# Soft-MoE attention kernel: batch-end rows stored by one transfer of 128 rows, two and a half early half-groups, last weight slab in row pieces of 4, 2, 1, 1

## Chip, cores, metric

One core of a Trainium2 chip. The metric is the device time of one execution in microseconds (us). Before the change: 181.42 us, median of 3 runs (181.19 to 181.47).

## The reference, cut to what matters

```python
attn_out = attention(q, k, v)                       # 8 batches, 8 heads, 576 tokens, 64 per head
x = attn_out.transpose(0, 2, 1, 3).reshape(4608, 512)
logits = x @ phi                                    # 32 slots: 8 experts of 4
slot_input = softmax(logits, over tokens).T @ x     # needs all tokens
for e in range(8):                                  # two matrices of 512 x 1024 for each expert
    slot_out[e] = relu(slot_input[e] @ w1[e]) @ w2[e]
return softmax(logits, over slots) @ slot_out       # 4608 x 512 float32, 9.4 MB
```

The output, 9.44 MB, can only be computed when the last expert's `w2` has arrived. So the kernel ends with a long stretch of stores: after about 150 us.

## The kernel before

Words used below: PE is the matmul engine (PEld its weight loads); DVE, ACT and POOL are the vector, scalar and GpSimd engines; SP issues the stores. SBUF is the on-chip memory of 128 partitions that the stores read, HBM the memory that they write. "DMA engines" are the 16 engines that move the data of all transfers.

The kernel computes attention batch by batch while a queue of transfers brings q, k, v and then the weights (cast to bf16 on the way). The last expert weights come as column slabs (`s` = 0 or 1: columns 0 to 255, 256 to 511), so that the left half of the output can start before the right half's weights are there:

```python
for s in range(2):
    wq += [w2_slab(6, s), w2_slab(7, s, 0, 4), w2_slab(7, s, 4, 2),
           w2_slab(7, s, 6, 2)]        # expert 7 in row pieces of 4, 2, 2
...
for x in (1, 2):                       # left, right columns
    l2((6,), x, ...)                   # matmuls with w2 of expert 6
    for y, cs in enumerate((range(4), range(4, 6), range(6, 8))):
        l2((7,), x, 256 * x - 256, 256, cs, [b_w2h[y][x - 1]])
    op(DVE, ... tensor_tensor(o_so ..., AluOp.add) ...)        # "the add" below, line 881
```

The output is then made in tiles of 128 tokens: one matmul, one eviction (ACT or DVE, in turn, copies the result to a float32 staging area in SBUF), and stores from there. Each batch has 576 = 512 + 64 tokens. A *group* G of 0 to 7 is the first 512 tokens of a batch: partition p holds tokens 4p to 4p + 3, so one row in memory is 4 x 2 KB = 8 KB, and the group is one 1 MB transfer of 128 rows. The eight *batch ends* of 64 tokens are gathered as a ninth group, 16 partitions for each batch, and stored by eight transfers:

```python
def tok(G, j):                                        # the columns (tokens) of tile j of group G
    return (a(o_et + 576 * G + j, [[4, 128]]) if G < 8 else a(o_tail + j, [[4, 128]]))

NA = 2                                                # groups 0, 1: stored by column halves
def store(G, c0, cw, prio, j0=0, n=4):
    for p0 in [0] if G < 8 else range(0, 128, 16):
        pn = 128 if G < 8 else 16
        dst = out[576 * G:576 * G + 512] if G < 8 else out[36 * p0 + 512:36 * p0 + 576]
        ...                                           # SP issues the transfer
```

Groups 0 and 1 are stored early: their left halves (four transfers of 256 KB, two tiles each, 1 KB rows) while the right slab of `w2` is still loading, their right halves after it. Then come group 2 (two transfers of 512 KB, 4 KB rows), groups 3 to 7 (1 MB each, 8 KB rows), and last the eight batch-end stores of 128 KB.

The softmax here doesn't subtract the row's maximum and nothing guards it: scores larger than these inputs give would overflow.

## Time and profile before

| | before |
|---|---|
| time, median | 181.42 us |
| span of the profiled run | 179.8 us |
| last weights landed | 152.3 us |
| add of the right half starts | 153.29 us |
| evictions done | 165.1 us |
| 8 KB packets, first start to last end | 161.24 to 178.97 us |

From the profile page of the kernel before: the span in 40 equal slices of 4.5 us. The first line is the busy share of the 16 DMA engines in tenths, the second what they moved.

```profile
DMA  5999999999999999999999999999999999799995
GB/s 184 233 210 211 214 209 213 215 208 213 213 210 215 212 209 210 215 211 208 215 211 211 215 210 214 214 214 211 215 211 213 197 196 235 243 401 408 425 346 162
```

The DMA engines are busy in nearly all slices. About 210 GB/s in the first 31 slices counts bf16 as written; the inputs that are read are float32, so twice as many bytes (the page: 30.41 MB in the load queue, 61.93 MB read from HBM). The stores then run at 400 to 425, and the last two slices fall to 346 and 162: the end of the stream is slow.

The windows view of the kernel before, for stretches of the store phase. The columns after the window are its length, then busy time and instructions of each engine, the clock granted to PE, the busy share of the DMA engines, and GB/s.

```profile
core 0: us, PE busy (x) PEld busy (x) DVE busy (x) ACT busy (x) POOL busy (x), PEclk, DMA share, GB/s
150.00:153.50 3.50, 3.25 (x18) 1.64 (x16) 1.10 (x4) 0.67 (x2) 0.00 (x0) 0.54 1.12 284
153.50:155.50 2.00, 1.73 (x12) 1.37 (x13) 1.49 (x5) 1.39 (x4) 0.00 (x0) 1.00 0.39 138
155.50:160.50 5.00, 4.84 (x18) 1.43 (x16) 5.00 (x9) 5.00 (x10) 0.00 (x0) 1.00 1.01 360
160.50:165.50 5.00, 2.29 (x8) 0.55 (x7) 4.60 (x7) 3.27 (x6) 0.00 (x0) 1.00 1.03 422
165.50:173.50 8.00, 0.00 (x0) 0.00 (x0) 0.00 (x0) 0.00 (x0) 0.00 (x0) 0.58 1.01 420
173.50:179.00 5.50, 0.00 (x0) 0.00 (x0) 0.00 (x0) 0.00 (x0) 0.00 (x0) 0.50 0.87 204
```

Read the last column. From 153.5 to 155.5 us the rate is 138: the early stores run out before the right half's stores can start. From 160.5 to 173.5 it is 420: rows of 8 KB. From 173.5 to 179 it is 204, and no compute engine has anything to do. These are the eight batch-end stores.

The transfers that write the output, from the DMA view: number, size, and median time from issue to landing.

```profile
out_dram<-ar SPq DMA_DIRECT2D x5, 1024.0 KB, 8.1
...
out_dram<-ar SPq DMA_DIRECT2D x8, 256.0 KB, 3.4
...
out_dram<-ar SPq DMA_DIRECT2D x2, 512.0 KB, 4.0
out_dram<-ar SPq DMA_DIRECT2D x8, 128.0 KB, 8.9
```

The timeline of the kernel before around the right half's add (start, length, engine, line, operation; in brackets the idle time before it and what ended it):

```profile
152.64 0.13 PEld L857 LDWEIGHTS ps<-ar 128*32 128x32 bf16 x2 [0.34 <-DMA ar<-in_moe_w_dram]
153.29 0.43 DVE L881 TENSOR_TENSOR ar<-ps,ar 64x256 bf16<-64x256 f32 x1 [2.40 <-PE ps L857]
...
153.77 9.16 PE L901 MATMUL ps<-ar 128*128 128x256 bf16 x36 [0.52 <-DVE ar L881]
```

Two matmuls (152.64) still had to run after the last weights, then the add (L881), then the output tiles (L901).

A word on packets. The trace records each packet of a transfer with its start, its time and its size; a store with 8 KB rows has one packet of 8,192 B for each row. Sorted by start, the 768 such packets fall into six blocks of 128, one for each megabyte. (The records do not name the engine that moved a packet, and the blocks are cut by count, so their borders blur where engines are apart.) In this kernel a block that runs smoothly has a mean packet of 314 to 319 ns: 128 packets on 16 engines, 8 for each on average, 2.5 us.

### The profile page before, as it was taken

How to read it: one execution, taken by the hardware profiler on the slowest of the kernel's cores; microseconds unless marked ns; L12 is line 12 of the kernel's file. 1: busy time of each engine (PE TensorE's matmuls, PEld its weight loads, DVE VectorE, ACT ScalarE, POOL GpSimd, SP SyncE). 2: the span in 40 equal slices, each digit the busy share in tenths (PEclk: the TensorE clock that was granted, in tenths of full speed). 3: DMA queues.
4: the chain of work that ended last, by engine and by line, in shares of the span. 5: the costliest groups of instructions: out<-in, count | busy, mean ns of one | idle time of the engine just before them, and what ended most of it. 6: DMA issues, size and time to landing. Idle time of an engine off the chain costs nothing.

```text
span 179.8 us, 4781 instructions
## 1 busy us (share of the span) xinstructions
PE 125.4 (70%) x2092; PEld 84.5 (47%) x2092; DVE 116.9 (65%) x219; ACT 104.9 (58%) x164; POOL 50.9 (28%) x101
## 2 busy tenths in 40 slices
PE   0008877987989899899789889885775469892000
PEld 0005645764767667666567667674431125420000
DVE  6898789779798798898699699291200104797000
ACT  2406598796798788787688788945020103794000
POOL 7559742242334134133930000951000000000000
PEclk9999999999999999999999999999999975999555
DMA  5999999999999999999999999999999999799995
GB/s 184 233 210 211 214 209 213 215 208 213 213 210 215 212 209 210 215 211 208 215 211 211 215 210 214 214 214 211 215 211 213 197 196 235 243 401 408 425 346 162
DMA packets 18900, 41.26 MB, mean 230 GB/s; under 512 B 1984, under 2 KB 8128, under 8 KB 17984
## 3 DMA queue, kind: packets, MB, share of 16 engines
q0 software_dynamic: 15024, 30.41, 89.6%
q1 hardware_dynamic: 3856, 10.55, 16.5%
q8 instruction: 16, 0.26, 0.5%
q14 instruction: 4, 0.03, 0.0%
HBM read 61.93 MB, written 9.44 MB: 397 GB/s over the span
## 4 chain that ended last, share of the span: by engine, by line
DMA 59%; DVE 20%; PE 6%; ACT 3%; issue 2%; POOL 2%; DVEq 0%
DMA ar<-in_k_dram 41%; DMA ar<-in_moe_w_dram 18%; DVE ar L488 6%; DVE ar L913 6%; DVE ar L614 2%; PE ps L857 2%; DVE ar L445 2%; PE ps L901 1%; POOL ar L371 1%; ACT ar L548 1%; DVE ar L450 1%; PE ps L509 1%; ACT ar L576 1%; ACT ar L670 1%; POOL ar L364 1%
## 5 line engine op out<-in xcount | busy, mean ns | idle before, releaser
L488 DVE STREAM_TRANSPOSE ar<-ar 128x576 uint32<-128x576 uint32 x40 | 48.5, 1239 | 7.7 <-DMA ar<-in_k_dram 7.7
L548 ACT ACTIVATE ar<-ps 128x1152 bf16<-128x1152 f32 (+1 forms) x32 | 38.0, 1186 | 20.6 <-PE ps L533 11.4
L509 PE MATMUL ps<-ar 128*128 128x320 bf16 (+1 forms) x128 | 22.7, 301 | 15.6 <-DVE ar L488 13.1
L614 DVE TENSOR_TENSOR ar<-ps,fs 96x768 bf16<-96x768 f32 (+1 forms) x32 | 26.3, 823 | 1.3
L576 ACT ACTIVATE ar<-ps 128x768 bf16<-128x768 bf16 x32 | 24.8, 810 | 2.2 <-PE ps L570 2.1
L509 PEld LDWEIGHTS ps<-ar 128*128 128x128 bf16 x128 | 10.5, 99 | 20.2 <-POOL ar L418 13.1
L570 PE MATMUL ps<-ar 128*128 128x128 bf16 x192 | 15.9, 229 | 3.8 <-DVE ar L614 3.4
L603 PE MATMUL ps<-ar 128*128 128x65 bf16 x320 | 14.7, 193 | 3.3 <-ACT ar L548 3.2
L910 ACT ACTIVATE ar<-ps,fs 128x512 f32<-128x512 f32 (+1 forms) x22 | 11.4, 656 | 8.7 <-PE ps L901 8.7
L857 PE MATMUL ps<-ar 128*32 128x512 bf16 (+1 forms) x80 | 11.7, 374 | 6.0 <-DMA ar<-in_moe_w_dram 5.4
L335 POOL DMA_DIRECT2D ar<-in_k_dram x16 | 8.9, 555 | 24.8 <-DVE ar L488 15.6
L570 PEld LDWEIGHTS ps<-ar 128*128 128x128 bf16 x192 | 12.4, 118 | 5.7 <-DVE ar L614 4.0
L603 PEld LDWEIGHTS ps<-ar 128*128 128x128 bf16 x320 | 12.0, 97 | 6.0 <-ACT ar L548 3.7
L913 DVE TENSOR_SCALAR ar<-ps,fs 128x512 f32<-128x512 f32 (+1 forms) x22 | 12.6, 649 | 1.3 <-PE ps L901 1.3
L364 POOL DMA_DIRECT2D ar<-in_moe_w_dram x12 | 6.4, 580 | 20.8 <-DVE ar L488 20.8
L335 POOL DMA_DIRECT2D ar<-in_q_dram x16 | 8.8, 547 | 10.5 <-DVE fs L610 5.0
L901 PE MATMUL ps<-ar 128*128 128x512 bf16 (+1 forms) x44 | 10.7, 372 | 1.4 <-DVE ar L881 1.1
L610 DVE RECIPROCAL fs<-ps 96x12 f32<-96x12 f32 (+1 forms) x32 | 6.2, 195 | 7.9 <-PE ps L603 7.6
L670 ACT ACTIVATE ar<-ps 128x576 bf16<-128x576 bf16 x16 | 9.6, 652 | 3.1 <-PE ps L654 3.1
L335 POOL DMA_DIRECT2D ar<-in_v_dram x16 | 8.8, 549 | 8.8 <-DVE fs L610 5.5
L857 PEld LDWEIGHTS ps<-ar 128*32 128x32 bf16 x80 | 5.0, 104 | 12.3 <-DMA ar<-in_moe_w_dram 8.8
L693 PE MATMUL ps<-ar 128*128 128x288 bf16 x64 | 9.2, 287 | 1.2 <-ACT ar L677 1.2
(75 smaller groups left out, 186.7 us busy)
## 6 DMA issues: line engine op xcount, KB each, us to landing
ar<-in_moe_w_dram POOLq DMA_DIRECT2D x29, 512.0 KB, 27.5
out_dram<-ar SPq DMA_DIRECT2D x5, 1024.0 KB, 8.1
ar<-in_k_dram POOLq DMA_DIRECT2D x16, 288.0 KB, 23.4
ar<-in_q_dram POOLq DMA_DIRECT2D x16, 288.0 KB, 23.5
ar<-in_v_dram POOLq DMA_DIRECT2D x16, 288.0 KB, 23.6
out_dram<-ar SPq DMA_DIRECT2D x8, 256.0 KB, 3.4
ar<-in_moe_w_dram SPq DMA_DIRECT2D x1, 1024.0 KB, 5.0
out_dram<-ar SPq DMA_DIRECT2D x2, 512.0 KB, 4.0
```

The source lines that it names most:

```text
L335: return pool.dma_start(a(o_stg + (s * 3 + j) * 1152, [[1, 1152]]), src[b, 4 * dl:4 * dl + 4].rearrange("h (p t) d -> (h p) (t d)", p=32))
L488: return dve.transpose(au(o_dst, [[1, 18], [18, 32]]), au(src, [[32, 18], [1, 32]]))
L509: pe.matmul(pf(h, 0, [[1, W]]), a(o_id, [[1, 128]]), a(msk, [[1, W]]), start=True, stop=False)
L548: eo = op(ACT, lambda P=P, W=W: act.activation(a(P, [[W, 4], [1, W]]), AP(ps, 0, [[4096, 128], [512, 4], [1, W]]), ACTF.Exp, scale=SCALE), ...
L570: last = pe.transpose(pb(bank.idx, bb * 256 + par * 32, [[64, 4], [1, 32]]), src, a(o_id, [[1, 128]]))
L576: op(ACT, lambda t=t, bank=bank: act.activation(a(o_vb[vs] + 3 * t * VBK, [[66, 12], [2, 32], [1, 2]]), pb(bank.idx, 0, [[64, 12], [1, 32] ...
L603: last = pe.matmul(pf(bank.idx + x, 65 * t, [[1, 65]]), w, a(VB + t * VBK + 66 * h, [[1, 65]]), start=True, stop=True)
L614: op(DVE, lambda hp=hp, bank=bank: dve.tensor_tensor(a(ox + 128 * hp, [[64, 2], [256, NT], [1, 64]], 0, rows), pf(bank.idx, 0, [[512, 2], ...
L857: last = pe.matmul(pf(sobank[x].idx, 0, [[1, n]], 32 * j, 32), a(o_htz + 1024 * g + 128 * c + 32 * j, [[1, 32]]), a(w2off(e) + DM * c + co ...
L901: op(PE, lambda: pe.matmul(pf(bank.idx, 0, [[1, cw]]), tok(G, j), a(o_so + c0, [[1, cw]]), start=True, stop=True), pet(1, cw), prio, reads ...
L910: op(ACT, lambda: act.activation(dst, src(), ACTF.Copy, scale=sca), actt(cw, .1), prio + .1, reads=[bank, b_rinv], writes=wr, name=f"OE{G} ...
L913: op(DVE, lambda: dve.tensor_scalar(dst, src(), sca, None, op0=AluOp.mult), dvet(cw, True) + .08, prio + .1, reads=[bank, b_rinv], writes= ...
```

## The change

The intent: the last stretch is taken to be slow because it consists of eight small transfers, so store all batch ends by one transfer of 128 rows of 8 KB, in the middle of the stream. Fill the hole at 154 us with a fifth early half-store ("two and a half groups by halves"). Let fewer matmuls wait for the last weights (row pieces of 4, 2, 1, 1). The diff, cut to its core:

```diff
-               w2_slab(7, s, 6, 2)]
+               w2_slab(7, s, 6, 1), w2_slab(7, s, 7, 1)]
...                                                  # POOL gathers the batch ends: partition p = 8 i + b
-        a(o_tail, [[64, 8], [1, 64]]), a(o_et + 512, [[576, 8], [1, 64]])), .8, T1 + 4, reads=[b_et],
+        a(o_tail, [[4, 8], [32, 16], [1, 4]]), a(o_et + 512, [[576, 8], [4, 16], [1, 4]])), .8, T1 + 4, reads=[b_et],
...
-        for y, cs in enumerate((range(4), range(4, 6), range(6, 8))):
+        for y, cs in enumerate((range(4), range(4, 6), range(6, 7), range(7, 8))):
...
-    NA = 2
+    NA = 2.5
...
-        for p0 in [0] if G < 8 else range(0, 128, 16):
-            pn = 128 if G < 8 else 16
-            dst = out[576 * G:576 * G + 512] if G < 8 else out[36 * p0 + 512:36 * p0 + 576]
...
+        if G < 8:
+            dst = out[576 * G:576 * G + 512, c0:c0 + cw].rearrange("(p j) f -> p j f", j=4)[:, j0:j0 + n, :]
+            src = af(ostg(G) + 2 * (512 * j0 + c0), [[512, n], [1, cw]])
+        else:
+            dst = out.rearrange("(b r) f -> b r f", b=8)[:, 512:576, :].rearrange("b (i j) f -> i b (j f)", j=4)
+            src = af(ostg(G), [[1, 2048]])
...                                                  # order: group 2, the batch ends, groups 3 to 7
+    for G, x in [(2, 2)] + [(G, x) for G in (8, 3, 4, 5, 6, 7) for x in (0, 2)]:
```

Partition 8i + b now holds tokens 4i to 4i + 3 of the end of batch b. In the destination, i (16 values, 8 KB apart) is the outer dimension and b (8 values, 1.18 MB apart) the inner one, because b and i cannot be one dimension of 128 with one step.

More of the change, by code (lines that the diff above doesn't have):

```diff
@@ L309, in bass_dilated_sliding_attn__then__soft_moe_slots_kernel @@
     b_w5h = [Buf(f"w5h{x}") for x in range(2)]
-    b_w2h = [[Buf(f"w2h{x}{s}") for s in range(2)] for x in range(3)]
+    b_w2h = [[Buf(f"w2h{x}{s}") for s in range(2)] for x in range(4)]
     b_htz, b_tail, b_so = Buf("htz"), Buf("tail"), [Buf("soA"), Buf("soB")]
@@ L373, in fn @@
                 moe_w2[e].rearrange("(p c) f -> p c f", c=8)[:, c0:c0 + n, 256 * s:256 * s + 256])
-        return (fn, n << 17, f"w2s_{e}{s}{c0}", [b_w2[e][s] if n == 8 else b_w2h[(0, 4, 6).index(c0)][s]])
+        return (fn, n << 17, f"w2s_{e}{s}{c0}", [b_w2[e][s] if n == 8 else b_w2h[(0, 4, 6, 7).index(c0)][s]])
     for e in range(8):
@@ L919, in store @@
               if c0 < 256 * (s + 1) and c0 + cw > 256 * s]
-        for p0 in [0] if G < 8 else range(0, 128, 16):
-            pn = 128 if G < 8 else 16
-            dst = out[576 * G:576 * G + 512] if G < 8 else out[36 * p0 + 512:36 * p0 + 576]
-            dst = dst[:, c0:c0 + cw].rearrange("(p j) f -> p j f", j=4)
-            store_ops.append(op(SP, lambda p0=p0, pn=pn, dst=dst: spq.dma_start(
-                dst[:, j0:j0 + n, :],
-                af(ostg(G) + 2 * (512 * j0 + c0), [[512, n], [1, cw]], p0, pn)), .1, prio, kind="dma",
-                nbytes=pn * n * cw * 4, rate=347e3 if cw < 512 else 420e3,
-                sem=sem(f"s_o{G}{c0}{j0}{p0}"), reads=rd, name=f"ST{G}{c0}{j0}{p0}"))
+        if G < 8:
[4 more added lines that the diff above has]
+            src = af(ostg(G), [[1, 2048]])
+        store_ops.append(op(SP, lambda: spq.dma_start(dst, src), .1, prio, kind="dma",
+                            nbytes=128 * n * cw * 4, rate=347e3 if cw < 512 else 420e3,
+                            sem=sem(f"s_o{G}{c0}{j0}"), reads=rd, name=f"ST{G}{c0}{j0}"))
     T2 = T1 + 40
@@ L939, in bass_dilated_sliding_attn__then__soft_moe_slots_kernel @@
         store(G, 256, 256, T2 + 10 + G + .25 * x + .2, x, 2)
-    for n in range(int(2 * NA), 18):
-        G, x = n // 2, n % 2 * 2
+    for G, x in [(2, 2)] + [(G, x) for G in (8, 3, 4, 5, 6, 7) for x in (0, 2)]:
+        at = G if G < 8 else 2.6
         for j in (x, x + 1):
-            out_tile(G, j, 0, 512, T2 + 10 + G + .25 * x)
-        if G == NA:
-            store(G, 0, 512, T2 + 10 + G + .25 * x + .2, x, 2)
+            out_tile(G, j, 0, 512, T2 + 10 + at + .1 * x)
+        if G < NA:
+            store(G, 0, 512, T2 + 10 + at + .1 * x + .1, x, 2)
         elif x:
-            store(G, 0, 512, T2 + 10 + G + .5)
+            store(G, 0, 512, T2 + 10 + at + .3)
     order = sc.run([4, 5, 6, 7], [0, 1, 2, 3], last_ex[0])
```

## The prediction

> **What bounds the kernel now.** The DMA engines: 90% busy or more in nearly all of the page's slices, and 59% of the chain of waits that ended last. They load until 152.3 us; from then on only stores are left. Store rates, by stretches of the trace:
> - first column-half stores (four of 256 KB): issued by 151.6, flowing until 155.0, below full rate from 153.5; around 155.0 to 155.5 nothing moves, because the second half's matmuls wait for the last w2 piece (152.6) and its add (153.29);
> - 1 KB rows (second halves) 348 GB/s, 4 KB rows (group 2) about 400, 8 KB rows (1 MB stores) 420, steady to 173.5;
> - then the eight batch-end stores of 128 KB[...]: 1.05 MB from 173.8 to 178.9 (208 GB/s), though six were issued by 172.2. At 420 GB/s these bytes take 2.5 us. Last landing 179.3, span 179.8.
>
> Compute ends at 165.1.
>
> **What the change does.**
> 1. One 1 MB transfer replaces the eight; its destination is 16 x 8 rows of 8 KB. [...] It moves to just after group 2, so the kernel ends with a plain 1 MB store. Worth 5.05 - 2.5 = 2.5 us, all on the path.
> 2. A fifth 256 KB store before the last w2 piece. It fills the hole of 153.5 to 155.5, where about 0.48 MB of capacity is unused. It is 0.75 us of DMA work at 348 GB/s; in return half of group 2's 512 KB store goes at 348 instead of 400 (+0.1 us). Net 0.5 to 0.8 us. It costs two matmuls (0.23 us each) before the L2 of the second half, where PE idled 0.34 us.
> 3. Row pieces 4, 2, 1, 1: one matmul, not two (0.62 us), after the last landing, 0.1 to 0.3 us off each add; this pays for point 2's delay. Two more POOL issues at 113 to 119 us, behind 30 us of queued transfers: free.
> 4. Strided batch-end copy on POOL (0.60 us now, perhaps 1): PE waits longer at 125 us, but its next weights land near 140. Free.
>
> **Sum.** Second-half stores flow from about 155.4 us; 1.31 MB at 348, 0.52 at 400, 6.29 at 420 GB/s are 20.1 us, so the last data go at 175.6 and the span ends near 176.5. Gain 3.2 us: 181.42 becomes about **178.2 us**, range 177.4 to 179.2 (8 in 10). Chances: faster by over 2% 0.30, within 2% 0.69, slower 0.01.
>
> **What would show it right or wrong.** Right: store rate near 420 GB/s until the last us; the merged store moving in about 2.5 us around 161 to 163; the rate no longer zero near 155; last add at about 153.2; compute done at about 165.
>
> **What would make it wrong.** The 128 KB stores may be slow not from their number but from where they write (128 KB in one stretch at a time); then the merged store would be slow too: 180.7. The fifth store could slow the last weight pieces and delay the add. The hole could close only on some engines, as others work until 155.0: then point 2 gives 0.3. If the second add comes earlier than I think, or the stream ends with less skew, 177.4.

The 3.2 us are 2.5 us of point 1, worked out from the rates of the trace, and about 0.7 us of point 2 (point 3 was to pay for its delay), and the sum came to 178.2 us. The recorded expectations below have cuts of the same kind.

## The result

| | before | changed |
|---|---|---|
| time, median of 6 runs each | 181.37 us | 180.80 us (180.65 to 181.03) |
| ratio of the changed to before | | 0.9972 (0.9959 to 0.9985) |
| span of the profiled run | 179.8 us | 179.0 us |
| add of the right half starts | 153.29 us | 152.95 us |
| first 8 KB packet starts | 161.24 us | 160.45 us |
| last 8 KB packet ends | 178.97 us | 178.22 us |
| between these two | 17.73 us | 17.77 us |

A ratio here and below is fast runs of one kernel over fast runs of the other in the same rounds, so it is not quite the ratio of the medians that are quoted. Executions over 1.5% slower than the fastest of the same kernel are left out of the means. The bracket is a 95% interval.

The kernel is 0.3% faster, not 1.8%. The last row of the table already says where the gain is missing: the six megabytes in 8 KB rows, which contain the batch ends in both kernels, take 17.7 us in both.

The slices of the changed kernel:

```profile
DMA  6999999999999999999999999999999999899996
GB/s 185 234 213 210 217 207 215 211 211 210 218 207 213 215 209 210 215 210 210 215 208 212 213 211 217 211 215 210 219 209 217 196 195 230 304 356 264 421 419 260
```

The end is somewhat better, but there is a new low of 264 GB/s in the fourth slice from the end. The windows view of the changed kernel, same columns and windows as before:

```profile
core 0: us, PE busy (x) PEld busy (x) DVE busy (x) ACT busy (x) POOL busy (x), PEclk, DMA share, GB/s
150.00:153.50 3.50, 2.62 (x17) 1.33 (x18) 0.94 (x3) 0.28 (x1) 0.00 (x0) 1.00 1.18 307
153.50:155.50 2.00, 1.82 (x13) 1.43 (x14) 1.61 (x5) 1.72 (x5) 0.00 (x0) 1.00 0.67 234
155.50:160.50 5.00, 4.86 (x19) 1.34 (x17) 5.00 (x10) 5.00 (x10) 0.00 (x0) 1.00 1.07 367
160.50:165.50 5.00, 1.73 (x6) 0.41 (x5) 4.00 (x7) 2.72 (x5) 0.00 (x0) 1.00 0.99 262
165.50:173.50 8.00, 0.00 (x0) 0.00 (x0) 0.00 (x0) 0.00 (x0) 0.00 (x0) 0.54 1.01 423
173.50:179.00 5.50, 0.00 (x0) 0.00 (x0) 0.00 (x0) 0.00 (x0) 0.00 (x0) 0.50 0.68 286
```

The hole (153.5 to 155.5) went from 138 to 234 GB/s, as intended. But from 160.5 to 165.5 the rate is 262 where it was 422, with the DMA engines busy all the time (0.99). That is the merged store. And the last window is not a full 420 up to a sharp end: worked out from the packet records, the rate was 425 until 176.5 us and then declined over 1.7 us. The DMA view of the changed kernel has six stores of 1 MB now, with 11.0 us from issue to landing where five had 8.1:

```profile
out_dram<-ar SPq DMA_DIRECT2D x6, 1024.0 KB, 11.0
...
out_dram<-ar SPq DMA_DIRECT2D x10, 256.0 KB, 3.8
...
out_dram<-ar SPq DMA_DIRECT2D x1, 512.0 KB, 4.0
```

The timeline of the changed kernel around the add:

```profile
151.20 1.71 PE L857 MATMUL ps<-ar 128*32 128x256 bf16 x8 [0.18 <-DMA ar<-in_moe_w_dram]
...
152.63 0.09 PEld L857 LDWEIGHTS ps<-ar 128*32 128x32 bf16 x1 [0.31 <-DMA ar<-in_moe_w_dram]
152.95 0.43 DVE L881 TENSOR_TENSOR ar<-ps,ar 64x256 bf16<-64x256 f32 x1 [2.44 <-PE ps L857]
...
153.44 1.29 PE L901 MATMUL ps<-ar 128*128 128x256 bf16 x10 [0.52 <-DVE ar L881]
...
154.92 7.41 PE L901 MATMUL ps<-ar 128*128 128x512 bf16 x25 [0.18 <-DVE ar L913]
```

The new piece of one row works: one matmul runs behind the last weights instead of two, and in this pair of profiles the add comes 0.34 us earlier, and the first tiles with it. But most of the 0.34 us is not the piece. The profile of the kernel before happened to have a granted PE clock of 0.54 from 150 to 153.5 us, the changed one 1.00 (windows above). merge_only, a run described below, keeps the two matmuls and had a clock of 1.00:

```profile
152.63 0.39 PE L857 MATMUL ps<-ar 128*32 128x256 bf16 x2 [0.29 <-DMA ar<-in_moe_w_dram]
153.06 0.43 DVE L881 TENSOR_TENSOR ar<-ps,ar 64x256 bf16<-64x256 f32 x1 [2.70 <-PE ps L857]
```

From the first of these matmuls to the add it took 0.43 us there, 0.65 in the kernel before and 0.32 in the changed one. So at the same clock the finer piece is worth 0.11 us, and the other 0.22 us belong to the clock of one profile. Evictions end 0.6 us earlier (164.5 instead of 165.1). What is left is to explain the slow merged store. Its packets (from the packet records, sorted by start, rows of 16; ns):

```
160.45  573 795 611 319 454 709 619 400 612 309 614 309 496 309 606 309
160.91  309 472 572 642 646 595 604 360 346 380 631 596 629 596 636 629
161.44  629 629 629 598 629 594 600 645 647 605 596 631 598 635 646 648
162.08  867 888 871 818 879 878 904 687 738 741 672 671 558 529 539 559
162.94  309 309 382 309 309 309 518 309 309 542 309 406 501 424 309 508
163.25  309 309 309 309 309 372 312 622 312 309 633 309 645 602 309 309
```

309 ns is the undisturbed packet, and 629 is about twice that. After a mixed start more than two rows of 16 are near 629: this looks like engines that move in step, 16 at a time, each at half its speed (inferred). A row of up to 904 ns follows, and then the pattern breaks up.

### The profile page after: what moved, and what is told of

It is laid out like the page before. It is cut to its first block, busy times and chain, and to the rows that moved or that the text cites. A ratio compares the mean times of both kernels' runs of the same rounds, so it can differ in the third digit from the quotient of the medians.

```text
span 179.0 us, 4780 instructions
## 1 busy us (share of the span) xinstructions
PE 127.9 (71%) x2093; PEld 87.5 (49%) x2094; DVE 118.0 (66%) x220; ACT 104.7 (58%) x165; POOL 51.7 (29%) x103
## 4 chain that ended last, share of the span: by engine, by line
DMA 32%; PE 23%; DVE 23%; ACT 6%; POOL 4%; issue 2%; DVEq 0%
DMA ar<-in_moe_w_dram 18%; DMA ar<-in_k_dram 15%; PE ps L509 7%; DVE ar L488 6%; DVE ar L913 6%; ACT ar L548 4%; POOL ar L371 4%; PE ps L603 3%; DVE ar L614 3%; PE ps L570 3%; PE ps L516 2%; PE ps L526 2%; PE ps L693 2%; DVE ar L494 2%; DVE ar L445 2%
## 5 line engine op out<-in xcount | busy, mean ns | idle before, releaser
L509 PE MATMUL ps<-ar 128*128 128x320 bf16 (+1 forms) x128 | 23.9, 313 | 15.4 <-DVE ar L488 13.1
L509 PEld LDWEIGHTS ps<-ar 128*128 128x128 bf16 x128 | 10.9, 102 | 20.1 <-POOL ar L418 13.1
L603 PE MATMUL ps<-ar 128*128 128x65 bf16 x320 | 15.7, 200 | 3.4 <-ACT ar L548 3.1
L603 PEld LDWEIGHTS ps<-ar 128*128 128x128 bf16 x320 | 12.9, 101 | 6.3 <-ACT ar L548 3.8
L570 PEld LDWEIGHTS ps<-ar 128*128 128x128 bf16 x192 | 12.8, 120 | 3.6 <-DVE ar L614 2.4
L857 PE MATMUL ps<-ar 128*32 128x512 bf16 (+1 forms) x80 | 10.5, 338 | 5.0 <-DMA ar<-in_moe_w_dram 3.5
L901 PE MATMUL ps<-ar 128*128 128x512 bf16 (+1 forms) x45 | 9.8, 339 | 1.5 <-DVE ar L881 1.0
```

Source lines behind the costliest of these rows:

```text
L509: pe.matmul(pf(h, 0, [[1, W]]), a(o_id, [[1, 128]]), a(msk, [[1, W]]), start=True, stop=False)
L570: last = pe.transpose(pb(bank.idx, bb * 256 + par * 32, [[64, 4], [1, 32]]), src, a(o_id, [[1, 128]]))
L603: last = pe.matmul(pf(bank.idx + x, 65 * t, [[1, 65]]), w, a(VB + t * VBK + 66 * h, [[1, 65]]), start=True, stop=True)
L857: last = pe.matmul(pf(sobank[x].idx, 0, [[1, n]], 32 * j, 32), a(o_htz + 1024 * g + 128 * c + 32 * j, [[1, 32]]), a(w2off(e) + DM * c + co ...
```

## Theories

These are conjectures; the runs below test them.

- **P, partitions.** How long a packet takes depends on which partitions are read at the same time: in some combinations the engines hold each other up. Which combinations was a guess, as no record names the engine of a packet. The measured packets would fit: plain stores have means of 314 to 319 ns; the merged store has rows of 16 near 629 ns, about 2 x 309, as if two engines took turns; the eight stores of before, which read 16 neighbours each, have 33 of their 128 packets over 900 ns, up to 1,466, as if up to four did. That the 16 x 8 form reads partitions 8 apart at the same time is part of the guess. Engines that get out of step would hold each other up less.
- **H, memory addresses.** The rows written together lie within one stretch of 128 KB (8 KB apart), or the next rows after them are 1.18 MB further on.
- **F, form.** The three-dimensional destination is itself slow.
- **N, number.** Before, eight small transfers were slow because each costs something; the merge removed that, and something else took its place.

## The experiments

Each run was timed beside fresh runs of the kernel before on the same chip (medians 181.36 to 181.55 us); runs of different rounds are best compared by their ratios to it.

### undo_merge: the change without the merged store

```diff
-    one 16 x 8 store after group 2, strided gather
+    the eight 16-row stores and the gather of before, last
```

> The fifth store and the finer weight pieces alone, with the eight batch-end stores of before, last. The trace after shows the last add 0.34 us earlier and the dip near 155 us filled, so these two parts alone should give 0.5 to 0.9 us: 180.5 to 180.9. If the merge itself gained nothing, this run is as fast as the changed kernel (180.8); if the merge gained the 0.5 us that its stretch of 4.6 us instead of 5.05 us suggests, this run is at 181.2; if the merge lost time through the uneven end that it leaves, this run is faster, 180.3.

180.95 us, ratio 0.9973 (0.9959 to 0.9987). The time is just above the expected 180.5 to 180.9. Without the merge the change is as good as with it (0.9972). The two small parts carry what was gained.

### merge_only: the merged store alone, in the kernel before

> The kernel before with only the merged batch-end store right after group 2. By the prediction alone it would be 2.5 us faster, 178.9. [...]three steps of 16 packets near 629 ns, then a mixed fourth, a stretch of 4.6 us, and an end that is uneven by 0.7 us; time 181.0 to 181.5, no different from before within 0.2%.

The second forecast is that of theory P; it carries over the packets of the changed kernel.

181.46 us, ratio 0.9994 (0.9982 to 1.0007). The merge by itself is worth nothing that can be told from noise. The blocks of 16 packets near 629 ns are there; the 8 KB packets take 17.80 us from first to last.

### fifth_only and pieces_only

```diff
-    NA = 2            # fifth_only: the kernel before, this and the condition of group 2's store
+    NA = 2.5
```

```diff
-               w2_slab(7, s, 6, 2)]      # pieces_only: the kernel before, with this and its matmuls
+               w2_slab(7, s, 6, 1), w2_slab(7, s, 7, 1)]
```

> The kernel before with only the fifth early store of 256 KB. If the hole near 155 us is what these two small parts gain from, 0.3 to 0.7 us: 180.7 to 181.1. If the gain of the run without the merge (0.47 us) came from the finer weight pieces, this run is within 0.15 us of before.

180.92 us, ratio 0.9968 (0.9955 to 0.9981).

> The kernel before with only the row pieces 4, 2, 1, 1. The add of the second half comes 0.2 to 0.3 us earlier, but the DMA engines that still work on the early stores until 155.0 do not finish sooner: 0 to 0.3 us, 181.1 to 181.4.

181.34 us, ratio 0.9993 (0.9979 to 1.0008). The fifth store alone gives all of the gain; the finer pieces bring the add a little earlier but do not clearly change the time. Both runs are inside their expected ranges.

### wide_16x8: six stores in the 16 x 8 form, rows 72 KB apart

The last six groups are all stored in the form of the merged store. In the destination the outer dimension steps by 72 KB instead of 8 KB, the inner one still by 1.18 MB. The rest of the kernel is that of pitch36 (below), so the two differ only in the form of these six stores.

```diff
+    if G > 2:
+        dst = out.rearrange("(b i g j) f -> g i b (j f)", b=8, i=16, g=9)[G]
+        src = af(ostg(G), [[1, 2048]])
```

> A wrong (permuted) result on purpose: the last six groups are all stored in the 16 x 8 form[...]. P and F: each of the six takes about 4.6 us instead of 2.5, so about 10 us slower than the changed kernel, near 191. H by closeness[...]: all fast, about 178. H by jumps of 1.18 MB: slow like P.

181.20 us, ratio 0.9990 (0.9972 to 1.0008). All four guesses missed. Against pitch36, 178.31 us, the form costs 2.9 us. (The rows of the output are so alike that the permutation is an error of 1.2%, worked out from the reference's output.) The windows of this run:

```profile
core 0: us, PE busy (x) PEld busy (x) DVE busy (x) ACT busy (x) POOL busy (x), PEclk, DMA share, GB/s
...
160.50:165.50 5.00, 1.91 (x6) 0.54 (x5) 4.08 (x7) 2.80 (x5) 0.00 (x0) 1.00 0.98 261
165.50:173.50 8.00, 0.00 (x0) 0.00 (x0) 0.00 (x0) 0.00 (x0) 0.00 (x0) 0.52 1.02 403
```

The first of the six stores is as slow as in the changed kernel (mean packet 528 ns against 518, the same steps of 16 near 629), though its rows are 72 KB apart and not 8: closeness in memory is not the cause. The second has 356 ns, the other four 316 to 322, though they have the same form and the same jumps of 1.18 MB: neither the form nor the jumps are slow in themselves. So the slowness seems to belong to engines that move in step, and to end when they have fallen out of step (inferred from the packet times, as the records do not name the engines; no run shows the drift itself). My expectation for P had left out that the slowness ends by itself after the first store or two. The end seems to pay instead: the last store took 3.7 us from first start to last end, although its mean packet was 316 ns, so some engines seem to finish late.

### merged_112: same memory rows, other partitions

Seven batch ends on 112 partitions (p = 7i + b, so one step of i is 7 partitions instead of 8), the eighth as one store of partitions 112 to 127.

```diff
-    a(o_tail, [[4, 8], [32, 16], [1, 4]])            # p = 8 i + b
+    a(o_tail, [[4, 7], [28, 16], [1, 4]])            # p = 7 i + b, b < 7
+    a(o_tail + 448, [[1, 64]])                       # p = 112 + i, b = 7
```

> Same form and same HBM rows, other SBUF partitions: seven batch ends from 112 partitions[...], and the eighth as 16 rows. Theory P [...]the 7-part transfer moves in about 2.5 us with most packets near 310 ns instead of 500 to 650, the 16-row one stays slow; the time is 0.7 to 1.2 us below the changed kernel, 179.6 to 180.1. Theory F (the 16 x n form) and theory H (HBM rows close together or 1.18 MB apart): packets stay at 500 to 650 ns, time stays 180.8 or a little worse.

180.42 us, ratio 0.9949 (0.9937 to 0.9962), 0.4 us better than the changed kernel's 180.8, less than P's 0.7 to 1.2. The packets show where. The first 96 packets have a mean of 398 ns instead of 529, and 13 of them instead of 53 are over 550 ns. The 16-row store behind it reads 16 neighbours, and eight packets there took 1,173 to 2,060 ns, which probably cost part of the gain (the longest are well over 4 x 309 ns; this stays open). Same memory rows and same kind of form, other partitions, other speed: that is for P, against H and F. Why steps of 7 are better than steps of 8 is not shown.

### halves_64: half of the partitions at a time

All-plain stores (the kernel of pitch36, below), but the last six groups are stored as two two-dimensional transfers of 64 partitions each, first the six of partitions 0 to 63, then the six of 64 to 127. Each memory row is the same.

```diff
+    part(0, 64, ...)                                 # now
+    late.append(lambda: part(64, 64, ...))           # after all groups' first parts
```

> The pitch-36 kernel (178.3 us), but the last six groups are each stored as two plain two-dimensional transfers of 64 partitions, all six of partitions 0 to 63 first, then all six of 64 to 127; same HBM rows of 8 KB, same sizes in all. Theory P: [...]packets near 620 ns, 6.3 MB at about 212 GB/s, 29.7 us instead of 14.8: about 193 us. Theories of form or of HBM addresses: packets stay near 310 to 320 ns, about 178.5.

193.02 us (one run, state unknown; the effect is 14.7 us). P had said about 193, the other theories 178.5, which is also near what pitch36 took (178.31). P's figure is an estimate, two packet times of 309 ns for every packet; why half of the partitions should double it was a guess, not shown before this run. The windows:

```profile
core 0: us, PE busy (x) PEld busy (x) DVE busy (x) ACT busy (x) POOL busy (x), PEclk, DMA share, GB/s
...
160.50:165.50 5.00, 1.90 (x6) 0.54 (x5) 4.07 (x7) 2.78 (x5) 0.00 (x0) 0.83 1.01 220
165.50:173.50 8.00, 0.00 (x0) 0.00 (x0) 0.00 (x0) 0.00 (x0) 0.00 (x0) 0.50 1.00 209
173.50:179.00 5.50, 0.00 (x0) 0.00 (x0) 0.00 (x0) 0.00 (x0) 0.00 (x0) 0.50 0.99 226
```

The engines are always busy, at half the rate: 6.29 MB from 160.5 to 190.4 us is 210 GB/s, and the means of the six blocks are 555 to 632 ns. There is no 16 x 8 form here, and no recovery like that of wide_16x8: the blocks stay slow. Nor is it the size of 512 KB: the two 512 KB stores of the kernel before, over 128 partitions, ran at about 400 GB/s (399 from 159 to 161 us).

### small_step8: the eight stores of before, with partitions 8 apart

The run without the merge, except that each 128 KB store reads partitions b, b + 8, ... b + 120 instead of 16 neighbours.

```diff
-    af(ostg(8), [[1, 2048]], p0, 16)
+    AP(ar_f.tensor, (p0 // 16 * NBF + ostg(8)) // 2, [[8 * NBF // 2, 16], [1, 2048]])
```

> The run without the merge (eight 128 KB stores, last), with one difference: each store reads 16 partitions in steps of 8 instead of 16 neighbours; HBM rows, sizes, number and order are the same. [...]no packets over 900 ns (but the transition), blocks of 16 near 629 ns as in the merged store, mean about 520 instead of 567 ns, time 0.2 to 0.6 us below that run's 180.95. If the number of transfers or the HBM rows set the time: unchanged pattern, 180.95.

The first forecast is that of theory P; it carries over the packets of the merged store.

180.04 us, ratio 0.9928 (0.9915 to 0.9940), 0.9 us below undo_merge's 180.95: more than the expected 0.2 to 0.6. (The two were timed in different rounds; their ratios to before, 0.9973 and 0.9928, have intervals that do not overlap.) First 64 packets of the last megabyte of each, in ns:

```
undo_merge (16 neighbours)
173.46  1331 1155 1227  948 1094  871 1151 1188 1098 1276  728  973  878 1071  924 1115
174.35   309  309  309  309  309  309  309  309 1446  309  309  309 1478  309  309  309
174.80  1364  309 1455  309 1138 1236 1465 1179 1124 1096 1175 1112 1125 1122 1171 1044
176.05   309  309  309  309  309  309  355  309  311  309  309  354  376  309  309  594
small_step8
173.10   825  558  422  429  309  616  731  382  619  309  581  309  520  309  518  309
173.59   612  309  426  634  509  589  636  322  631  332  608  606  348  642  631  642
174.04   624  624  622  622  589  611  589  642  631  632  609  642  631  700  694  748
174.67   885  884  887  887  882  845  906  751  802  724  673  660  574  608  532  559
```

Under P's guess, four engines that take turns need about 4 x 309 = 1,236 ns for a packet and two about 2 x 309, an estimate from the undisturbed packet of 309 ns. Not all packets are slow: of undo_merge's 128, 33 took over 900 ns and 81 less than 400. In their first 64 packets the eight small stores with steps of 8 show the pattern of the one merged store, with the same mean of 601 ns; after that they are quicker (354 against 435 ns). So theory N falls as the main cause: the stores are still eight, with the same memory rows and in the same order, and only other partitions made them faster.

### pitch36: no batch ends

If every partition owns 36 consecutive tokens (128 x 36 = 4608), there are no batch ends: nine groups, each a plain store of 128 rows of 8 KB, 72 KB apart. The row sums are taken once at the end by 36 one-column matmuls (PE waits for weights soon after anyway: 1.49, 0.55 and 1.40 us between 135.5 and 142 us in the kernel before). As the comparison would hardly notice swapped rows, correctness of the order rests on the code: token 36p + 4G + j is read, and row 36p + 4G + j is written.

```diff
-        return (a(o_et + 576 * G + j, [[4, 128]]) if G < 8 else a(o_tail + j, [[4, 128]]))
+        return a(o_et + 4 * G + j, [[36, 128]])
...
+        dst = out.rearrange("(p g j) f -> g p j f", g=9, j=4)[G][:, j0:j0 + n, c0:c0 + cw]
```

> No batch ends at all: each partition owns 36 consecutive tokens, so all nine groups are plain 128-partition stores of 8 KB rows at a pitch of 72 KB. P, F and H alike: no slow stretch, 8 KB packets near 310 ns throughout, time about 178.0 (the prediction's sum), 177.5 to 178.5. If the 72 KB pitch itself is slow in HBM, it is above 180.

178.31 us, ratio 0.9831 (0.9818 to 0.9844). The sum of the prediction had been 178.2. The windows:

```profile
core 0: us, PE busy (x) PEld busy (x) DVE busy (x) ACT busy (x) POOL busy (x), PEclk, DMA share, GB/s
...
153.50:155.50 2.00, 1.82 (x13) 1.62 (x14) 1.58 (x5) 1.70 (x5) 0.00 (x0) 1.00 0.69 243
...
160.50:165.50 5.00, 1.86 (x6) 0.54 (x5) 4.03 (x7) 2.75 (x5) 0.00 (x0) 1.00 1.01 418
165.50:173.50 8.00, 0.00 (x0) 0.00 (x0) 0.00 (x0) 0.00 (x0) 0.00 (x0) 0.60 1.01 420
173.50:179.00 5.50, 0.00 (x0) 0.00 (x0) 0.00 (x0) 0.00 (x0) 0.00 (x0) 0.54 0.34 143
```

418 and 420 GB/s, and it is over at 175.6. All six blocks have means of 314 to 318 ns, and the 8 KB packets take 15.22 us from first to last, against 17.73 before and 17.77 in the changed kernel.

### pitch36_alone, and more early stores

pitch36_alone is pitch 36 with the early stores and weight pieces of before.

> The pitch-36 layout with the two early halves groups and the weight pieces of before (no fifth store, no finer pieces): what a conflict-free batch-end store is worth by itself. The prediction's term for it was 2.5 us; the difference between pitch 36 and the changed kernel says 2.5 us too. Expected 2.4 to 2.8 us below before, 178.7 to 179.1, and the fifth store's share (0.5 us) still missing against pitch 36 (178.3).

178.80 us, ratio 0.9858 (0.9844 to 0.9871): 2.56 us below before, as expected. The 2.5 us that the prediction gave to the merge do exist; the merge did not collect them.

> Pitch 36 with six early 256 KB stores instead of five. In pitch 36 the rate is about half between 154.0 and 155.5 (190 to 250 GB/s), so half of the engines still have no work there; a sixth store would fill 0.26 MB of about 0.25 MB missing. 0.1 to 0.4 us faster: 177.9 to 178.2. It may be the same if the engines that are still busy are the ones that set the end.

177.75 us, ratio 0.9801 (0.9788 to 0.9815), a little better than the expected 177.9 to 178.2.

> Seven early stores: more than the hole holds, and two more 256 KB go at 348 instead of 400 GB/s (0.2 us lost). 177.9 to 178.6, about as pitch 36; the output matmuls before the second L2 (14 of 0.13 to 0.23 us) may delay the last add by some 0.3 us.

177.98 us, ratio 0.9821 (0.9804 to 0.9837). This is inside the expected range. Six early stores have the lowest median of the versions run, about 2.0% below before (at a bar of 2% that is unclear); seven are not better, and the intervals of the two overlap.

| run | us | ratio to before | first to last 8 KB packet, us |
|---|---|---|---|
| before | 181.37 | | 17.73 |
| the change | 180.80 | 0.9972 | 17.77 |
| merge_only | 181.46 | 0.9994 | 17.80 |
| undo_merge | 180.95 | 0.9973 | 17.65 |
| merged_112 | 180.42 | 0.9949 | 17.40 |
| wide_16x8 | 181.20 | 0.9990 | 18.47 |
| small_step8 | 180.04 | 0.9928 | 16.96 |
| pitch36_alone | 178.80 | 0.9858 | 15.24 |
| pitch36 | 178.31 | 0.9831 | 15.22 |
| pitch36_na3 | 177.75 | 0.9801 | 15.25 |
| halves_64 (one run) | 193.02 | | 29.89 |

## Why the prediction was wrong

- **What bounds the kernel: right.** The stores at the end, at 420 GB/s with 8 KB rows and half of that for the batch ends (204 GB/s).
- **Point 1, the merge: the step that failed.** The prediction said: "Worth 5.05 - 2.5 = 2.5 us, all on the path." It gained nothing clear of noise (merge_only, 0.1 us, ratio 0.9994). No idle engines show: the DMA share is 0.99 from 160.5 to 165.5 us. What failed is the step from busy engines to 2.5 us, that is, to 420 GB/s: in that window they moved 262. The merged store's mean packet was 518 ns against 314. At 8 packets for each engine, on average, this is 4.14 us instead of 2.51, 1.6 us lost; the store behind it lost 0.2 (342 ns), and the uneven end 0.7 (the last store took 3.45 us from first start to last end, a smooth one 2.7). Together 2.5 us, which is the gain that was forecast. That the partitions decide is shown most cleanly by small_step8, where they are all that differs between the stores; merged_112 and halves_64, in which number and size of the transfers differ too, agree. Why some combinations of partitions are slow is not shown by any run; which partitions the 16 x 8 form reads together is inferred from the like packets of small_step8 (601 ns over the first 64 in both), as the records do not name the engine.
- **The warning that named the outcome.** The prediction allowed for the merged store being slow too ("180.7") but gave it as reason "where they write". The size was right (180.80), the reason wrong, so the hit is partly luck: wide_16x8 moved the rows from 8 to 72 KB apart and changed nothing (528 ns), small_step8 left the rows and changed much (180.95 to 180.04 us).
- **Point 2, the fifth store: right.** "Net 0.5 to 0.8 us"; fifth_only measured 0.63 us between the medians (ratio 0.9968). The hole closed only partly, as suspected (138 to 234 GB/s), yet the gain did not fall to the 0.3 us that the prediction tied to that.
- **Point 3, the pieces: right on the add at equal clock, small in time.** The adds came 0.40 and 0.34 us earlier (147.93 to 147.53 and 153.29 to 152.95), but the two profiles differ in the clock that PE was granted; at a clock of 1.00 one matmul less is worth 0.11 us, at the low end of "0.1 to 0.3". The "0.62 us" for two matmuls was read at the low clock, too. The time of pieces_only is within noise of before.
- **Point 4, the strided copy: right.** 0.63 us instead of 0.60. PE waited 0.2 us for it at about 126 us, as it had before, and nothing waited at the end.
- **The sum:** with the batch ends free of conflicts and the two other parts as they are, the kernel takes 178.31 us; 178.2 had been worked out.

What stays open: small_step8 pays less (16.96 us for its 8 KB packets) than the merged store in mid-stream (17.77), though the first 64 packets have the same pattern. They differ in place as well as in number, and no run separates the two. Also, the end of the loads wandered between profiles (152.1 to 152.8 us) without relation to the edits, which is why the timed runs, and not single profiles, decide about parts of a microsecond.

## What to carry to other kernels

In these runs a transfer over 128 partitions was not fast by itself: it mattered which partitions were read at the same time (mean packets of 518 and 314 ns), for a reason that they do not show. Look at the packet times, where whole multiples of the usual one (629, and 924 to 1,478 in undo_merge, against 309 ns here) may hint at how many engines hold each other up. When small transfers are slow, change one property at a time (number, memory rows, partitions) before paying for a merge: coalescing eight stores of 128 KB into one of 1 MB was worth nothing here (ratio 0.9994), while changing only the partitions that the eight stores read was worth 0.9 us (180.95 to 180.04). Of the length of rows: in the kernel before, 1 KB rows were stored at 349 GB/s (155.7 to 158.7 us), 4 KB rows at 399 (159 to 161) and 8 KB rows at 420 (163.5 to 173.5). A layout without remainders (36 tokens for each partition) made the special case disappear, and with it 2.5 us that no rearrangement of the remainder had recovered.
